# Weights, gathers and head-pair products in the expert loop of an attention and mixture-of-experts kernel: another order, and two PSUM banks at a time

## The chip, the cores and the metric

The kernel runs on one core of a Trainium2 chip. The metric is the device time of one execution in microseconds (us). A core has five engines that run at the same time and wait for each other by semaphores: PE multiplies matrices, DVE and ACT do elementwise work, POOL (GpSimd) issues most of the transfers here, and SP issues the rest. Sixteen DMA engines move the data. Each engine works through its own instructions in the order in which they are written.

## What is computed

```python
# q, k, v: 8 batches x 8 heads x 576 positions x 64; N = 4608 tokens, D = 512, E = 8 experts, F = 1024
q_s = exp(q - max_d) / sum_d                     # softmax over the 64 features
k_s = exp(k - max_s) / sum_s                     # softmax over the 576 positions
kv  = einsum('bhsd,bhse->bhde', k_s, v)          # 64 x 64 for each batch and head
x   = einsum('bhsd,bhde->bhse', q_s, kv)         # then laid out as x[N, 512]
for e in range(8):                               # the expert of a token is hash(token_ids) % 8
    out[mask_e] = relu(x[mask_e] @ w1[e]) @ w2[e]
```

## The kernel before

The kernel sorts the tokens by expert before it makes x. Each expert has 640 slots in five blocks: eight cells of 72 slots, one for each batch (576 slots, the last block holds 64 of them), and 64 overflow slots. POOL fetches the q rows of an expert by an indirect transfer for each block (`gather`, five tiles `raw`). ACT takes their exponential into `qs` (`expq`), DVE sums and scales them in two parts, blocks 0 to 2 and 3 to 4 (`sums`), PE transposes them (`turn`, into PSUM tile `pq`) and DVE copies them to `qT`. The products of `qT` with the batches' matrices `kvr` (`product`, into PSUM tile `px`) give the transposed x, and ACT and DVE, by turns, cast them to the tile `XT`. A product covers two heads (a head pair, four of them) and, in the loop, two experts at a time.

An expert is then computed in eight pieces of its first layer (`first`: 8 matmuls on `w1r` into the PSUM tile `ph`, two pieces for each of four pairs of feature rows, columns 0 to 319 and then 320 to 639), each followed by ACT's `relu` into `hT`, and five output blocks (`second`: 8 matmuls on `w2r` into `po`), each followed by DVE's `result` into one of four buffers `ob` and by POOL's indirect `scatter` of that block to the output.

Up to and with experts 0 and 1 all of this stands in one list (`ORDER`), by short names: W21 is the fetch of w1 of expert 2, S1_0 the scatter of block 0 of expert 1, A and R a piece of a first layer and its relu. Experts 2 to 7 are computed by a loop. A pass of the loop has thirteen slots, one after each of the eight pieces and the five blocks, and hangs the work for later experts into them (`sl.at(slot, ...)`, slots 0 to 7 after pieces, 8 to 12 after blocks):

- ahead of everything else in the pass: the weights of the next expert, w1 in two halves and w2 in two halves, and then the five gathers of expert e + 3;
- slots 0 to 9: sums, scaling and transposes of expert e + 2;
- in odd passes (3 and 5) slots 8 to 12: products and casts of experts e + 1 and e + 2, in three groups of cells (0 to 2, 3 to 5, 6 to 7) with four head pairs each;
- slots 8 to 12: one exponential of expert e + 3 on ACT in each.

PSUM has eight banks: `ph` takes two pairs of banks (tag S, two banks a tile), `pq` and `px` share two single banks (tag Q), and `po` has two single banks (tag T). Weights are in two sets of buffers, for even and odd experts, so that w1 of expert e + 2 can only be fetched when the first layer of expert e is through.

Of the kernel before, what the change touches and what calls it, by code (L numbers as in the profile page):

```python
# [13 lines left out]
F32 = mybir.dt.float32  # L14
F16 = mybir.dt.float16
# [275 lines left out]
class _Attention:  # L291
# [61 lines left out]

    def gather(self, idx, widths, i):
        nc = self.nc
        q16 = self.q16s[i]
        raws = []
        for i, w in enumerate(widths):
            raw = self.qpool.tile([128, D_MOE], F32, tag="qraw", bufs=10)
            nc.gpsimd.indirect_dma_start(  # L360
                out=raw[0:w, :], out_offset=None, in_=self.q[:, :],
                in_offset=bass.IndirectOffsetOnAxis(ap=idx[0:w, i:i + 1], axis=0),
                bounds_check=N_TOK - 1, oob_is_err=False)
            raws.append(raw)
        return raws, q16, widths
# [26 lines left out]

    def turn(self, rq16, i):
        nc = self.nc
        q16, w = rq16[1], rq16[2][i]
        pq = self.ps.tile([128, 512], F32, tag="Q")
        pv = pq[:].bitcast(F16).rearrange("p (r t) -> p r t", r=8)[:, 0:NPAIR, 0:w]
        for r in range(NPAIR):
            nc.tensor.transpose(pv[:, r, :], q16[0:w, i, 2 * r:2 * r + 2, :].rearrange("p h d -> p (h d)"),  # L399
                                self.ident[0:w, 0:w])  # L400
        return pv
# [37 lines left out]
class _Moe:  # L439
# [4 lines left out]

    def fetch(self, w, e, what):
        src = self.w1 if what == 1 else self.w2
        for i in range(2):
            self.nc.gpsimd.dma_start(w[what - 1][:, 2048 * i:2048 * i + 2048], src[e, :, 2048 * i:2048 * i + 2048])  # L448
# [182 lines left out]
class _Steps:  # L631
# [35 lines left out]
def kernel(  # L667
# [13 lines left out]
    with ExitStack() as fctx:  # L681
# [17 lines left out]
        with tc.manual_schedule(engines={eng.Pool, eng.PE, eng.DVE, eng.Activation}):  # L699
# [20 lines left out]

            def gather(e):
                return at.gather(ix.gidx[:, e, :], QW, e if e < 2 else 1 - e % 2)

# [32 lines left out]

            def fetch(e, what):
                if what == 1:
                    wts[e] = moe.new_weights(wb if e % 2 else wa)
                moe.fetch(wts[e], e, what)  # L760

            for e in (0, 1, 2):
                for what in (1, 2):
                    add(f"W{e}{what}", fetch, e, what)
            for e in (0, "O", 1, 2, 3, 4):
# [76 lines left out]

            def turned(rq, e, i):
                V(qT[:, :, e % 4, 128 * i:128 * i + QW[i]], at.turn(rq, i))

            for e in range(2, E_MOE):
                h, w = hs[e % 2], wts[e]
                if e + 1 < E_MOE:
                    fetch(e + 1, 1)
                    fetch(e + 1, 2)  # L850
                sl.clear()
                X = None

                def softened(ee):
                    rq = qs[ee]
                    sl.at(0, lambda: sl.at(2, at.sums(rq, 0, 3)))
                    sl.at(3, lambda: sl.at(5, at.sums(rq, 3, 5)))
                    for i, t in enumerate((5, 6, 7, 9, 9)):
                        sl.at(t, lambda i=i: turned(rq, ee, i))

                def products(ee, es, t):
                    for (lo, hi), s in zip(((0, 3), (3, 6), (6, 8)), t):
                        for r in range(NPAIR):
# [71 lines left out]
```

## Time and profile before

| | |
|---|---|
| median of 3 runs | 246.99 us (246.44 to 248.87) |
| the profiled execution | 246.38 us |
| span of its trace, first to last instruction | 244.5 us |
| PE busy | 195.6 us, 80% of the span |
| DVE, ACT, POOL busy | 139.2, 114.4 and 113.8 us |
| mean granted TensorE clock | 0.983 of 2.4 GHz |
| chain that ended last | PE 49%, DMA 33% of the span |

The profiled execution spends 1.88 us outside its span. Until about 87 us the chain runs through transfers; from there to 237.7 us it runs on PE, with a few pieces of other engines and of transfers between. The loop over experts 2 to 7 begins at 116.5 us.

### The profile page before, as it was taken

Reading aid. Unit: us, or ns where it says so; the run is one execution under the profiler, and the core shown is the slowest. Engines: PE = TensorE matmul, PEld = TensorE weight load, DVE = VectorE, ACT = ScalarE, POOL = GpSimd, SP = SyncE. Lnnn points to the kernel's source line nnn. Section 1 sums busy time; section 2 is a strip of 40 time slices with the busy share of each in tenths; the row PEclk is TensorE's granted clock in tenths of the full one; section 3 lists DMA queues with packets and bytes.
Section 4 is the critical chain, followed back from the end, with each engine's and each line's share of the span. In section 5 each row is a group of like instructions: output and inputs, shape, how many; then the busy total and the mean of one; then the engine's idle time right before and its main releaser. Section 6 shows DMA issues by size and latency. Waiting matters only on the chain.

```text
span 244.5 us, 4885 instructions
## 1 busy us (share of the span) xinstructions
PE 195.6 (80%) x1955; PEld 128.0 (52%) x1955; DVE 139.2 (57%) x274; ACT 114.4 (47%) x181; POOL 113.8 (47%) x140
## 2 busy tenths in 40 slices
PE   2536605729659989999999895799999899999980
PEld 2436605617534565665764563367557556647530
DVE  7895438291883799835854584279359552031140
ACT  8533337856951892480441650456166234505400
POOL 6170341635434628834884585068753226043051
PEclk9999999999998999999999999799999999999998
DMA  6999999999999728795599499529988924982032
GB/s 220 323 328 314 415 327 286 323 260 251 214 212 279 247 87 157 246 188 178 117 213 300 164 182 247 188 95 181 237 305 165 218 101 106 212 226 88 1 129 79
DMA packets 13548, 51.42 MB, mean 210 GB/s; under 512 B 2504, under 2 KB 2504, under 8 KB 12496
## 3 DMA queue, kind: packets, MB, share of 16 engines
q0 software_dynamic: 12224, 41.58, 68.3%
q1 hardware_dynamic: 1296, 9.47, 9.8%
q8 instruction: 17, 0.28, 0.5%
q14 instruction: 11, 0.09, 0.1%
HBM read 63.25 MB, written 10.49 MB: 302 GB/s over the span
## 4 chain that ended last, share of the span: by engine, by line
PE 49%; DMA 33%; issue 5%; DVE 5%; POOL 3%; ACT 2%; POOLq 0%; ACTq 0%; DVEq 0%
PE ph L462 22%; PE po L474 22%; DMA raw<-in_q_dram,gidx 17%; DMA v<-in_v_dram 9%; DMA w2r<-in_moe_w_dram 7%; PE px L410 3%; PE pq L399 2%; POOL raw L360 2%; DVE A L127 1%; ACT qs L371 1%; ACT hT L467 1%; DVE ob L480 1%; ACT XT L810 1%; DVE EV L107 0%; POOL w1r L448 0%
## 5 line engine op out<-in xcount | busy, mean ns | idle before, releaser
L462 PE MATMUL ph<-XT,w1r 128*128 128x320 f16 (+2 forms) x512 | 75.6, 303 | 1.1 <-ACT hT L467 1.1
L474 PE MATMUL po<-w2r,hT 128*128 128x512 f16 x320 | 75.3, 387 | 0.0
L484 POOL DMA_INDIRECT out_dram<-ob,sidx x40 | 40.5, 1013 | 66.8 <-DVE ob L480 61.1
L467 ACT ACTIVATE hT<-ph 128x640 f16<-128x640 f32 (+2 forms) x64 | 44.8, 703 | 43.4 <-PE ph L462 43.2
L480 DVE TENSOR_SCALAR ob<-po 128x512 f32<-128x512 f32 x40 | 27.6, 690 | 61.0 <-PE po L474 56.6
L462 PEld LDWEIGHTS <-w1r 128*128 128x128 f16 x512 | 49.8, 99 | 21.3 <-issue 1.6
L360 POOL DMA_INDIRECT raw<-in_q_dram,gidx x40 | 44.6, 1114 | 30.9 <-issue 6.6
L474 PEld LDWEIGHTS <-hT 128*128 128x128 f16 x320 | 30.8, 100 | 34.0 <-issue 3.1
L371 ACT ACTIVATE qs<-raw 128x512 f16<-128x512 f32 (+1 forms) x44 | 26.3, 626 | 26.5 <-DMA raw<-in_q_dram,gidx 26.3
L383 DVE TENSOR_REDUCE rq<-qs 128x16 f32<-128x1024 f16 (+1 forms) x18 | 26.1, 1450 | 5.2 <-ACT qs L371 5.1
L399 PE MATMUL pq<-ident,qs 128*128 128x128 f16 (+1 forms) x176 | 16.4, 228 | 12.8 <-DVE qs L389 11.9
L389 DVE TENSOR_TENSOR qs<-qs,rq 128x1024 f16<-128x1024 f16 (+1 forms) x18 | 26.2, 1455 | 0.3
L338 PE MATMUL pt<-v,k 64*64 64x65 f16 x576 | 15.0, 222 | 10.6 <-ACT v L328 10.6
L410 PE MATMUL px<-qT,kvr 128*128 128x144 f16 (+1 forms) x160 | 14.6, 224 | 10.8 <-ACT XT L810 4.6
L399 PEld LDWEIGHTS <-qs 128*128 128x128 f16 (+1 forms) x176 | 12.3, 103 | 17.0 <-issue 10.3
L810 ACT CAST XT<-px 128x288 f16<-128x288 f32 (+1 forms) x26 | 11.6, 453 | 20.5 <-PE px L410 20.4
L338 PEld LDWEIGHTS <-k 64*64 64x64 f16 x576 | 14.5, 136 | 11.2 <-issue 10.7
L410 PEld LDWEIGHTS <-kvr 128*128 128x128 f16 x160 | 11.5, 103 | 16.2 <-issue 11.2
L324 ACT ACTIVATE k<-kraw 128x2304 f16<-128x2304 f32 x8 | 16.9, 2118 | 2.4 <-PE pt L338 1.7
L810 DVE CAST XT<-px 128x288 f16<-128x288 f32 (+1 forms) x26 | 13.2, 518 | 6.8 <-PE px L410 6.8
L448 POOL DMA_DIRECT2D w1r<-in_moe_w_dram x16 | 9.3, 596 | 7.2 <-PE px L410 4.7
L448 POOL DMA_DIRECT2D w2r<-in_moe_w_dram x16 | 8.9, 576 | 2.3 <-DMA v<-in_v_dram 1.6
(102 smaller groups left out, 110.4 us busy)
## 6 DMA issues: line engine op xcount, KB each, us to landing
kraw<-in_k_dram SPq DMA_DIRECT2D x8, 1152.0 KB, 10.2
w1r<-in_moe_w_dram POOLq DMA_DIRECT2D x16, 512.0 KB, 7.7
w2r<-in_moe_w_dram POOLq DMA_DIRECT2D x16, 512.0 KB, 11.3
v<-in_v_dram POOLq DMA_DIRECT2D x8, 594.0 KB, 17.1
raw<-in_q_dram,gidx POOLq DMA_INDIRECT x40, 10.5
out_dram<-ob,sidx POOLq DMA_INDIRECT x40, 3.2
raw<-in_q_dram,oidx POOLq DMA_INDIRECT x4, 15.5
ids<-in_moe_token_ids_dram SPq DMA_DIRECT2D x1, 36.0 KB, 1.7
```

Source lines behind the costliest of these rows:

```text
L338: nc.tensor.matmul(pkv[s, r, 0:DH_ + 1], lhsT=k16[s, r * C9 + c, :], rhs=v16[s, r * C9 + c, 0:DH_ + 1], start=(c == 0), stop=(c == C9 - 1))
L360: nc.gpsimd.indirect_dma_start(out=raw[0:w, :], out_offset=None, in_=self.q[:, :], in_offset=bass.IndirectOffsetOnAxis(ap=idx[0:w, i:i + 1 ...
L371: self.nc.scalar.activation(q16[0:w, i].rearrange("p h d -> p (h d)"), raws[i][0:w, :], ACT.Exp)
L389: nc.vector.tensor_tensor(out=qf, in0=qf, in1=rv.rearrange("p i h -> p (i h)").unsqueeze(2) .to_broadcast([w, (hi - lo) * H_, DH_]), op=AL ...
L399: nc.tensor.transpose(pv[:, r, :], q16[0:w, i, 2 * r:2 * r + 2, :].rearrange("p h d -> p (h d)"), self.ident[0:w, 0:w])
L410: nc.tensor.matmul(pv[:, :, i * CELL:(i + 1) * CELL], lhsT=self.kvrs[b][:, r, :], rhs=qT[:, r, q0 + es.start:q0 + es.stop, b * CELL:(b + 1 ...
L462: nc.tensor.matmul(ph[:, i, :hi - lo], lhsT=w1r[:, dc, fc * 128:(fc + 1) * 128], rhs=XTp[:, e % 2, dc, lo:hi], start=(dc == 0), stop=(dc = ...
L467: self.nc.scalar.activation(hT[:, 2 * f2:2 * f2 + 2, lo:hi], ph[:, :, :hi - lo], ACT.Relu)
L474: nc.tensor.matmul(po[:], lhsT=hT[:, fc, blk * 128:(blk + 1) * 128], rhs=w2r[:, fc, :], start=(fc == 0), stop=(fc == FC - 1))
L480: self.nc.vector.tensor_scalar(out=ob[:], in0=po[:], scalar1=1.0 / SX, scalar2=None, op0=ALU.mult)
L484: sc = self.nc.gpsimd.indirect_dma_start(out=self.out[:, :], out_offset=bass.IndirectOffsetOnAxis(ap=self.ix.sidx[:, e, blk:blk + 1], axis=0),
L810: (V if r % 2 else A)(X[:, es, r, lo * CELL:hi * CELL], px[e, r, lo])
```

## The change

Five things change, all but one of them in the loop:

1. The gathers of expert e + 3 stand first in a pass, and the two halves of w2 of expert e + 1 are put between them, after the second and after the fourth gather.
2. The two halves of w1 are fetched two experts ahead (w1 of e + 2 in pass e) in slots 8 and 10, behind the scatters of blocks 0 and 2. For this, w1 of expert 3 (W31) is fetched in the list ahead of the loop, behind the last piece of expert 1's first layer and ahead of expert 1's scatters.
3. The products of the loop write two head pairs into one tile of two banks (`products`, tag S, shared with `ph`), and one cast takes both: pairs 0 and 1 by ACT, pairs 2 and 3 by DVE.
4. The groups of products stand in slots 8, 10 and 11, whole, instead of being spread over 8 to 12.
5. `turn` transposes up to two blocks into one bank, followed by one copy: blocks 0 and 1 in slot 5, block 2 in slot 6, blocks 3 and 4 in slot 8 (before: slots 5, 6, 7, 9 and 9).

The matmuls are the same in number and shape (PE has 5012 rows in both orders).

```diff
-    def gather(self, idx, widths, i):
+    def gather(self, idx, widths, i, between={}):
...
         for i, w in enumerate(widths):
+            if i in between:
+                between[i]()
...
+    def products(self, qT, h, lo, hi, es, q0):
+        nc = self.nc
+        px = self.ps.tile([128, 2, 512], F32, tag="S")
+        n, ne = hi - lo, es.stop - es.start
+        pv = px[:, :, 0:ne * n * CELL].rearrange("p r (e i) -> p e r i", e=ne)
+        for r in range(2):
+            for i in range(n):
+                b = lo + i
+                nc.tensor.matmul(pv[:, :, r, i * CELL:(i + 1) * CELL], lhsT=self.kvrs[b][:, 2 * h + r, :],
+                                 rhs=qT[:, 2 * h + r, q0 + es.start:q0 + es.stop, b * CELL:(b + 1) * CELL],
+                                 start=True, stop=True)
+        return pv
...
-PP2_01 TP3_3 EQ4_2 PC2_01 A1_0_3 TC3_3 R1_0_1 PP2_00 TP3_4 R1_0_3 A1_288_2 TC3_4 PC2_00 EQ4_0 PP2_61 PP2_60
+PP2_01 TP3_3 EQ4_2 PC2_01 A1_0_3 TC3_3 R1_0_1 PP2_00 TP3_4 R1_0_3 A1_288_2 TC3_4 W31 PC2_00 EQ4_0 PP2_61 PP2_60
...
             for e in range(2, E_MOE):
                 h, w = hs[e % 2], wts[e]
-                if e + 1 < E_MOE:
-                    fetch(e + 1, 1)
-                    fetch(e + 1, 2)
...
-                    for i, t in enumerate((5, 6, 7, 9, 9)):
-                        sl.at(t, lambda i=i: turned(rq, ee, i))
+                    for i, n, t in ((0, 2, 5), (2, 1, 6), (3, 2, 8)):
+                        sl.at(t, lambda i=i, n=n: turned(rq, ee, i, n))
...
-                        for r in range(NPAIR):
-                            sl.at(s + r // 2, lambda r=r, lo=lo, hi=hi: (
-                                prod(ee, es, r, lo, hi), prodc(ee, es, r, lo, hi)))
+                        for h in range(2):
+                            sl.at(s, lambda h=h, lo=lo, hi=hi: (A, V)[h](
+                                X[:, es, 2 * h:2 * h + 2, lo * CELL:hi * CELL],
+                                at.products(qT, h, lo, hi, es, ee % 4 - es.start)))
...
-                        products(e + 1, slice(0, 2), (8, 9, 11))
+                        products(e + 1, slice(0, 2), (8, 10, 11))
+                w2 = {2 * i + 2: lambda i=i: fetch(e + 1, 2, (i,)) for i in range(2)}
                 if e + 3 < E_MOE:
-                    qs[e + 3] = gather(e + 3)
+                    qs[e + 3] = gather(e + 3, between=w2)
+                elif e + 1 < E_MOE:
+                    for f in w2.values():
+                        f()
+                if e + 2 < E_MOE:
+                    for i in range(2):
+                        sl.at(8 + 2 * i, lambda i=i: fetch(e + 2, 1, (i,)))
```

Line numbers move: 360 becomes 362, 448 becomes 465, 484 becomes 501, 480 becomes 497, 371 becomes 373, 844 becomes 860, and the casts of the loop go from line 810 to line 877. On POOL, the queue of pass 3 in the loop, from its first instruction to its last scatter, before (`w1r` and `w2r` are weights, `raw` gathered q rows, `out_dram` the output):

```order
L448 DMA w1r<-in_moe_w_dram 128x2048 x2
L448 DMA w2r<-in_moe_w_dram 128x2048 x2
L360 DMA raw<-in_q_dram,gidx 128x512 x4
L360 DMA raw<-in_q_dram,gidx 64x512
L484 DMA out_dram<-ob,sidx 4608x512 x5
```

and the same pass on POOL now:

```order
L362 DMA raw<-in_q_dram,gidx 128x512 x2
L465 DMA w2r<-in_moe_w_dram 128x2048
L362 DMA raw<-in_q_dram,gidx 128x512 x2
L465 DMA w2r<-in_moe_w_dram 128x2048
L362 DMA raw<-in_q_dram,gidx 64x512
L501 DMA out_dram<-ob,sidx 4608x512
L465 DMA w1r<-in_moe_w_dram 128x2048
L501 DMA out_dram<-ob,sidx 4608x512 x2
L465 DMA w1r<-in_moe_w_dram 128x2048
L501 DMA out_dram<-ob,sidx 4608x512 x2
```

The first gather stood behind four halves of weights and now stands behind none of its own pass; the halves of w1 moved to stand among the scatters.

On ACT, behind the relus of pass 3, before (`qs` from `raw` is an exponential, `XT` from `px` a cast of products):

```order
L810 CAST XT0_265<-px_2352 128x2x216
L371 ACTIVATE qs1_106<-raw_2210 128x512
L810 CAST XT0_265<-px_2389 128x2x216
L810 CAST XT0_265<-px_2399 128x2x216
L371 ACTIVATE qs1_106<-raw_2214 128x512
L810 CAST XT0_265<-px_2424 128x2x216
L371 ACTIVATE qs1_106<-raw_2218 128x512
L810 CAST XT0_265<-px_2449 128x2x144
L371 ACTIVATE qs1_106<-raw_2222 128x512
L810 CAST XT0_265<-px_2472 128x2x144
L371 ACTIVATE qs1_106<-raw_2226 64x512
```

and now:

```order
L877 CAST XT0_265<-px_2356 128x2x2x216
L373 ACTIVATE qs1_106<-raw_2204 128x512
L373 ACTIVATE qs1_106<-raw_2208 128x512
L877 CAST XT0_265<-px_2405 128x2x2x216
L373 ACTIVATE qs1_106<-raw_2213 128x512
L877 CAST XT0_265<-px_2437 128x2x2x144
L373 ACTIVATE qs1_106<-raw_2217 128x512
L373 ACTIVATE qs1_106<-raw_2222 64x512
```

Six casts became three of twice the width; the second one has two exponentials ahead of it, where it had one.

On DVE, from the second output block of pass 3 on, before (`ob` from `po` is the result of a block, `qT` from `pq` a copy of transposes):

```order
L480 TENSOR_SCALAR ob_2372<-po_2363 128x512
L844 COPY qT_263<-pq_2377 128x4x128
L844 COPY qT_263<-pq_2383 128x4x64
L810 CAST XT0_265<-px_2394 128x2x216
L810 CAST XT0_265<-px_2404 128x2x216
L480 TENSOR_SCALAR ob_2419<-po_2410 128x512
```

and now, from the first output block of that pass on:

```order
L497 TENSOR_SCALAR ob_2341<-po_2332 128x512
L860 COPY qT_263<-pq_2346 128x4x192
L877 CAST XT0_265<-px_2364 128x2x2x216
L497 TENSOR_SCALAR ob_2385<-po_2376 128x512
L497 TENSOR_SCALAR ob_2400<-po_2391 128x512
L877 CAST XT0_265<-px_2413 128x2x2x216
```

The copy of blocks 3 and 4 moved from behind the second result to behind the first one, and two more results now stand between it and the cast of the second group of products.

## Rows read from the trace of the kernel before

**Rows 1.** Busy time of each engine, granted clock, DMA share: before the loop; passes 3, 4, 5.

```profile
86.90:116.46 29.56, 29.55 (x220) 18.27 (x220) 21.75 (x40) 14.97 (x27) 15.93 (x16) 1.00 0.67 169
...
135.01:162.39 27.38, 22.48 (x157) 13.94 (x156) 14.27 (x24) 11.76 (x20) 13.28 (x15) 0.94 0.69 177
162.39:180.94 18.55, 18.55 (x128) 11.24 (x125) 12.38 (x21) 9.04 (x15) 13.05 (x14) 1.00 0.91 228
180.94:202.89 21.95, 20.87 (x157) 13.39 (x156) 14.41 (x24) 8.67 (x15) 7.67 (x10) 1.00 0.68 161
```

**Rows 2.** The chain in pass 3: start, us, what.

```profile
141.87 11.37 DMA raw<-in_q_dram,gidx
...
153.32 0.63 ACT qs L371
...
154.41 0.88 PE px L410 x6
155.29 2.94 PE po L474 x8
158.23 0.38 PE px L410 x6
```

**Rows 3.** What PE waited for, 100 to 245 us: total us, times, longest.

```profile
PE px L410 <- ACT XT L810: 3.9, 2, 3.5
PE px L410 <- DVE qT L844: 1.3, 2, 0.7
PE ph L462 <- ACT hT L467: 0.8, 1, 0.8
```

**Rows 4.** Busy time, granted clock, DMA share in pass 3, right behind the long wait.

```profile
154.40:158.05 3.65, 3.64 (x14) 1.75 (x14) 0.61 (x1) 1.05 (x2) 0.00 (x0) 0.56 0.52 178
```

**Rows 5.** The chain in pass 5, columns as above.

```profile
196.36 0.64 PE px L410 x6
197.00 1.73 PE po L474 x8
```

**Rows 6.** Landing of the five gathers of pass 3, issued from 141.9 us on.

```profile
DMA to landing us min/median/max: 9.0/10.3/11.4
```

**Rows 7.** Pass 6 while weights alone are moved: DMA share, GB/s in the last columns.

```profile
210.00:212.00 2.00, 2.00 (x15) 1.32 (x14) 0.00 (x0) 1.24 (x3) 0.00 (x0) 1.00 1.06 215
```

**Rows 8.** Landing of the last of five gathers issued at 99.4 us.

```profile
DMA to landing us min/median/max: 3.5/3.5/3.5
```

**Rows 9.** Casts and exponentials by form, 116 to 205 us.

```profile
L371 ACT ACTIVATE qs<-raw 128x512 f16<-128x512 f32 x12 | 7.6, 631 | 19.3 <-DMA raw<-in_q_dram,gidx 19.1
...
L810 DVE CAST XT<-px 128x432 f16<-128x432 f32 x8 | 4.8, 603 | 5.0 <-PE px L410 5.0
...
L810 ACT CAST XT<-px 128x432 f16<-128x432 f32 x8 | 4.1, 517 | 10.8 <-PE px L410 10.8
```

**Rows 10.** Cost on POOL of issuing half of w1: busy us and mean ns of one, all 16.

```profile
L448 POOL DMA_DIRECT2D w1r<-in_moe_w_dram x16 | 9.3, 596 | 7.2 <-PE px L410 4.7
```

**Rows 11.** Landing of the scatter of block 0 of expert 2, issued at 128.7 us.

```profile
DMA to landing us min/median/max: 8.5/8.5/8.5
```

**Rows 12.** DVE in order of time: last result of expert 1, scaling and last result of pass 2.

```profile
116.66 0.69 DVE L480 TENSOR_SCALAR ob<-po 128x512 f32<-128x512 f32 x1 [1.03 <-PE po L474]
...
119.59 1.76 DVE L389 TENSOR_TENSOR qs<-qs,rq 128x1536 f16<-128x1536 f16 x1
...
123.75 1.21 DVE L389 TENSOR_TENSOR qs<-qs,rq 128x1024 f16<-128x1024 f16 x1
...
137.37 0.69 DVE L480 TENSOR_SCALAR ob<-po 128x512 f32<-128x512 f32 x1 [3.20 <-PE ph L462]
```

**Rows 13.** Scatter of block 0 of expert 1: issue and landing.

```profile
L484 POOL DMA_INDIRECT out_dram<-ob,sidx x1: 1028/1028/1028, 109.7 to 109.7; - x1
...
DMA to landing us min/median/max: 3.7/3.7/3.7
```

**Rows 14.** PE in order of time, pass 2: its first transposes.

```profile
122.98 0.39 PE L399 MATMUL pq<-ident,qs 128*128 128x128 f16 x4
```

More of the change, by code (lines that the diff above doesn't have):

```diff
@@ L391, in sums, with turn @@
         return scale
-    def turn(self, rq16, i):
+    def turn(self, rq16, i, n=1):
         nc = self.nc
-        q16, w = rq16[1], rq16[2][i]
+        q16, w = rq16[1], rq16[2]
         pq = self.ps.tile([128, 512], F32, tag="Q")
-        pv = pq[:].bitcast(F16).rearrange("p (r t) -> p r t", r=8)[:, 0:NPAIR, 0:w]
-        for r in range(NPAIR):
-            nc.tensor.transpose(pv[:, r, :], q16[0:w, i, 2 * r:2 * r + 2, :].rearrange("p h d -> p (h d)"),
-                                self.ident[0:w, 0:w])
-        return pv
+        pv = pq[:].bitcast(F16).rearrange("p (r t) -> p r t", r=NPAIR)
+        for j in range(i, i + n):
+            o = 128 * (j - i)
+            for r in range(NPAIR):
+                nc.tensor.transpose(pv[:, r, o:o + w[j]], q16[0:w[j], j, 2 * r:2 * r + 2, :]
+                                    .rearrange("p h d -> p (h d)"), self.ident[0:w[j], 0:w[j]])
+        return pv[:, :, 0:sum(w[i:i + n])]
     def product(self, qT, r, lo, hi, es, q0=0):
@@ L443, in __init__, with fetch @@
         self.out, self.ix, self.ps = out, ix, ps
-    def fetch(self, w, e, what):
+    def fetch(self, w, e, what, halves=(0, 1)):
         src = self.w1 if what == 1 else self.w2
-        for i in range(2):
+        for i in halves:
             self.nc.gpsimd.dma_start(w[what - 1][:, 2048 * i:2048 * i + 2048], src[e, :, 2048 * i:2048 * i + 2048])
@@ L719, with gather @@
             ix.core(cpool, lambda: at.fill(ix))
-            def gather(e):
-                return at.gather(ix.gidx[:, e, :], QW, e if e < 2 else 1 - e % 2)
+            def gather(e, **kw):
+                return at.gather(ix.gidx[:, e, :], QW, e if e < 2 else 1 - e % 2, **kw)
             st = _Steps()
@@ L755, with fetch @@
             add("GO", lambda: qs.update(O=at.gather(oidx, [128] * NBP, 0)))
-            def fetch(e, what):
-                if what == 1:
+            def fetch(e, what, halves=(0, 1)):
+                if e not in wts:
                     wts[e] = moe.new_weights(wb if e % 2 else wa)
[L760 to L764, printed above, removed]
+                moe.fetch(wts[e], e, what, halves)
+            for e, what in ((0, 1), (0, 2), (1, 1), (1, 2), (2, 1), (2, 2), (3, 1)):
+                add(f"W{e}{what}", fetch, e, what)
             for e in (0, "O", 1, 2, 3, 4):
@@ L841, with turned @@
             sl = _Slots()
-            def turned(rq, e, i):
-                V(qT[:, :, e % 4, 128 * i:128 * i + QW[i]], at.turn(rq, i))
+            def turned(rq, e, i, n):
+                V(qT[:, :, e % 4, 128 * i:128 * i + sum(QW[i:i + n])], at.turn(rq, i, n))
             for e in range(2, E_MOE):
                 h, w = hs[e % 2], wts[e]
-                if e + 1 < E_MOE:
-                    fetch(e + 1, 1)
-                    fetch(e + 1, 2)
                 sl.clear()
@@ L857, in softened @@
                     sl.at(3, lambda: sl.at(5, at.sums(rq, 3, 5)))
-                    for i, t in enumerate((5, 6, 7, 9, 9)):
-                        sl.at(t, lambda i=i: turned(rq, ee, i))
+                    for i, n, t in ((0, 2, 5), (2, 1, 6), (3, 2, 8)):
+                        sl.at(t, lambda i=i, n=n: turned(rq, ee, i, n))
                 def products(ee, es, t):
                     for (lo, hi), s in zip(((0, 3), (3, 6), (6, 8)), t):
-                        for r in range(NPAIR):
-                            sl.at(s + r // 2, lambda r=r, lo=lo, hi=hi: (
-                                prod(ee, es, r, lo, hi), prodc(ee, es, r, lo, hi)))
+                        for h in range(2):
+                            sl.at(s, lambda h=h, lo=lo, hi=hi: (A, V)[h](
+                                X[:, es, 2 * h:2 * h + 2, lo * CELL:hi * CELL],
+                                at.products(qT, h, lo, hi, es, ee % 4 - es.start)))
                 if e + 2 < E_MOE:
@@ L869 @@
                         X = XTs[(e + 1) // 2 % 2]
-                        products(e + 1, slice(0, 2), (8, 9, 11))
+                        products(e + 1, slice(0, 2), (8, 10, 11))
+                w2 = {2 * i + 2: lambda i=i: fetch(e + 1, 2, (i,)) for i in range(2)}
                 if e + 3 < E_MOE:
-                    qs[e + 3] = gather(e + 3)
+                    qs[e + 3] = gather(e + 3, between=w2)
[5 more added lines that the diff above has]
+                        sl.at(8 + 2 * i, lambda i=i: fetch(e + 2, 1, (i,)))
+                if e + 3 < E_MOE:
                     for i in range(5):
```

## The prediction

> **What bounds the kernel now.** I read the busy time by stretch first. In the 29.56 us ahead of the loop PE is busy for 29.55 [rows 1], so nothing is to be had there but by less work on PE. In the loop, pass 4 keeps PE busy for all of its 18.55 us; passes 3 and 5 take 27.38 and 21.95 us [rows 1]. They hold the same pieces and blocks and, on top, the products: 32 matmuls. Six of those take 0.38 us [rows 2], so 32 take 2.0 us, and an odd pass without a wait would take 18.55 + 2.0 = 20.55 us. Pass 3 is 6.83 us above that and pass 5 is 1.40 us: 8.2 us in which PE stands or crawls. All else in the loop is PE at work.
>
> The list of PE's waits says for what: casts of products by ACT (3.9 us, one of 3.5), copies of transposes by DVE (1.3 us, two waits) and a relu (0.8) [rows 3]. The chain names the cause of the largest. The first gather of pass 3 is under way for 11.37 us, the exponential that waits for it starts at 153.32, and only behind it can ACT cast the products whose bank PE needs for the next ones, at 154.41 [rows 2]. The wait has a tail: right behind it the granted clock is 0.56 of full speed, a mix of the 1.2 and 2.4 GHz levels [rows 4]; the next block takes 2.94 us where one takes 1.73 [rows 2, 5], and six products 0.88 instead of 0.38 [rows 2]: 1.7 us. Adding up pass 3: 0.8 + 0.7 + 3.5 + 1.7 = 6.7, the 6.83 to within the small gaps. The relu that PE waits for early in this pass stands on ACT behind late exponentials too, those of pass 2's gathers.
>
> **The change part by part.**
>
> *Gathers first.* In pass 3 the five gathers land 9.0 to 11.4 us after issue [rows 6]: they are issued behind four halves of weights, which are moved first. A half is 512 KB; where weights alone are moved they go at 215 GB/s [rows 7], 2.44 us a half, 9.8 us for four. The last gather of an earlier group, issued when the weights ahead of it were through, landed in 3.5 us [rows 8]. Now the first two gathers have no weights of their own pass ahead of them, the last has two halves: between 3.5 and 3.5 + 2 x 2.44 = 8.4 us. They are also issued sooner, since four issues of weights at 0.6 us [rows 10] no longer stand ahead. POOL is through with the last scatter of expert 2 some 2 us after PE begins pass 3 at 135.0, so the first two go out by 138.5 and the last, with three gathers and two halves between, at about 143.5; they land by about 144 (3.5 us and one half left over) and 152. ACT needs the first two when PE comes to the third group of products, which reuses the banks of the second: 9.9 us of pieces and transposes (18.55 less five blocks of 1.73), four blocks and two groups, so from 135.0 + 9.9 + 6.9 + 1.5 = 153.3, and less a cast, 152. It needs the last at the end of the pass, 135.0 + 20.55 = 155.6. That leaves 8 and 3.6 us. So the 3.5 us, the 1.7 us of low clock behind it and the 0.8 go. Nothing on ACT is late in their place: it is busy for 11.76 us of this pass [rows 1].
>
> *Transposes in slots 5, 6, 8.* The two waits for DVE were for the copy of blocks 3 and 4, made in slot 9 directly ahead of the products that read it. The copy now comes in slot 8, two blocks or 3.5 us ahead. Slot 8 needs the scaling of blocks 3 and 4, over at 123.75 + 1.21 = 124.96 in pass 2 [rows 12], and comes after the pieces and one block, at about 127.7. One of these waits is in pass 3, the other in pass 5; there 3.9 - 3.5 = 0.4 us for ACT's cast between groups [rows 3] goes with it, as the groups no longer stand directly behind one another in two banks. Worth the 1.4 us of pass 5 and the 0.7 already counted in pass 3.
>
> *Two head pairs a cast.* ACT takes 0.517 and DVE 0.603 us for 432 columns [rows 9]. A cast of 864 is at most two of these, 1.03 and 1.21, and not less than one. I take the upper end, which costs nothing: between the groups in slots 10 and 11 lies a block of 1.73 us, in which ACT has one exponential (0.63 [rows 9]) and a cast (1.03). DVE has a result (0.69 [rows 12]) and a cast (1.21) in 1.73 + 0.75. The two-bank tiles are shared with the first layer: the products of slot 8 wait for the last relus, and the next pass's first pieces for the casts of slot 11, each with a block between. The matmuls are the same. Value 0, between 0 and +1.2 (four handovers at 0.3, if that cover fails).
>
> *w1 among the scatters.* Two halves, 1.2 us of POOL's time [rows 10], now stand between five scatters of 1.03 us [rows 13]: 6.4 us in the 8.65 of five blocks. Their own wait is for a first layer that is over. Each scatter behind a half lands up to 2.44 us later. A buffer `ob` is used again after four blocks, so block 4 waits for the scatter of block 0. That happened before: the scatter of expert 2's block 0 took 8.5 us [rows 11], and DVE began block 4's result only at 137.37 [rows 12], without a wait of PE for it. Now it has two halves ahead, not four, issued sooner. Value 0.
>
> *W31 ahead of the loop.* Here something gets worse. On POOL W31 waits for expert 1's last piece, with expert 1's scatters behind it; that piece is over well before their first result. But w1 of expert 3 is now moved ahead of those scatters. The one of block 0 landed at 109.7 + 3.7 = 113.4 [rows 13]; two more halves make that 118.3. The last result of expert 1 needs its buffer and began at 116.66 [rows 12], so DVE starts pass 2's sums 1.6 us late. The scaling that ended at 119.59 + 1.76 = 121.35 [rows 12] then ends at 123.0; PE transposes at 122.98 [rows 14]. The slack just covers it: +0.1, between 0 and +1.2 (if a half takes 3 us).
>
> Sum: -6.8 - 1.4 + 0.1 = -8.1 us against the profiled execution of 246.38: **238.3 us**. That execution is 0.6 us below the median; the forecast stays with it, and the difference goes into the range. The end of the program (the last scatter) is not touched.
>
> **The rivals.**
>
> *DMA becomes the bound.* Pass 4 has a DMA share of 0.91 over 18.55 us [rows 1]: 16.9 us of work, and passes 2 to 4 now follow at 18.55, 20.55 and 18.55. For it: only 1.7 us are to spare in an even pass. Against it: the work per pass stays the same and is spread more evenly. If the mix runs 20% slower, a pass needs 20.3 us, and passes 2 and 4 lose 1.7 each: 241.7. The Trainium skill (DMA: Bandwidth & Descriptors, Specifications) gives a limit of about 358 GB/s of HBM traffic for a core; by it a half, read as 1 MB of fp32, would take an estimated 2.9 us, an even pass's transfers some 18.3 us, the queue would hardly ever run empty, and this rival would have 0.3. The trace does not bear it out: 215 GB/s written in 16 bit [rows 7] is 430 GB/s read.
>
> *The change does not do what it says: the gathers stay late.* If they take 11.4 us [rows 6] still, the second lands at 150 and the last at 155, and each of three passes loses up to 1 us: 239.5 to 241. Against it: the 3.5 us [rows 8].
>
> *The shared banks bind.* If exponentials come in a burst, ACT has two (1.26) and a cast (1.03) ahead of the products of slot 11, 2.3 us in 1.73: 0.6 at each handover, 239.3 to 240.7.
>
> *Slower than before: scatters.* If the scatters of block 0 are held up among the weights, DVE, which works in order, waits for a buffer, and the sums for the next transposes are late. It decides from about 8.5 us of landing: 6.9 us (four blocks) until the buffer is needed and 1.6 us of slack. At 13 us, half as much again as the worst seen [rows 11], each of passes 2 to 4 would lose 4.5 us and 1.7 of low clock behind it, as in pass 3: 238.3 + 3 x 6.2 = 256.9. Against it: with all four halves ahead it was 8.5.
>
> **How the numbers follow.** The forecast, all waits gone but for tenths, has 0.76 (237.4 to 239.2); late gathers 0.08; shared banks 0.06; DMA 0.06; scatters 0.02; anything else 0.02. The runs before reach 2.4 us above their lowest. The range, with these cases and the ends of the unknown costs, is 237.2 to 241.4. One per cent, 2.5 us, is about what a measurement of this kernel can tell from no change. All but the last two cases gain more than that: faster 0.95, same 0.03, slower 0.02.
>
> **What would show it.** In the profile after: passes 3 and 5 at about 20.5 us each with PE busy throughout; no wait of PE for casts or copies of over 0.3 us; gathers landing in 3 to 8 us; no granted clock below 1.00 in the loop; pass 2 at 18.5 to 19.7; casts of 864 columns at 1.0 to 1.2 us. The prediction is wrong if pass 2 or 4 grows by over a microsecond (DMA or W31), or if ACT still waits for gathers between its casts.

## Result and profile after

The changed kernel takes 240.32 us in the median of 4 runs (239.44 to 242.1), the kernel before 247.93 (246.44 to 249.55, 4 runs). The ratio is 0.970, with an interval from 0.961 to 0.979. The profiled execution took 239.44 us with a span of 237.7, against 246.38 and 244.5 before. Here and below a ratio leaves out the executions that ran in a slower state of the chip (over 1.5% above the fastest of the same kernel).

The first view to read is the busy time by stretch, for passes 2 to 5 and for what follows the last matmul. The columns are busy us of PE, PE's weight loads, DVE, ACT and POOL, then granted clock, DMA share and GB/s.

```profile
116.66:136.70 20.04, 18.71 (x125) 11.16 (x124) 11.38 (x16) 8.56 (x13) 13.27 (x15) 1.00 0.76 199
136.70:157.25 20.55, 20.55 (x158) 13.24 (x156) 14.48 (x19) 10.65 (x16) 14.91 (x15) 1.00 1.02 244
157.25:175.79 18.54, 18.54 (x125) 11.25 (x124) 11.98 (x18) 7.93 (x12) 13.67 (x14) 1.00 0.91 206
175.79:196.55 20.76, 20.71 (x158) 13.24 (x156) 14.32 (x19) 8.66 (x12) 8.04 (x10) 1.00 0.88 202
...
231.30:237.70 6.40, 0.07 (x1) 0.00 (x0) 0.69 (x1) 0.00 (x0) 1.30 (x2) 0.67 0.22 78
```

Against [rows 1], pass 3 went from 27.38 to 20.55 us and pass 5 from 21.95 to 20.76, with PE busy throughout; pass 4 stayed; the granted clock is 1.00 in all four. Pass 2, which runs from 116.46 to 135.01 before, 18.55 us, grew to 20.04, and there PE is idle for 1.33 us. From the start of the loop to the end of the span it is 121.04 us, 128.04 before. The sum: -6.83 (pass 3), -1.19 (pass 5), +1.49 (pass 2), -0.5 (the end, 6.90 us before), and the loop begins 0.2 us later: -6.8, which is 237.7 - 244.5.

What PE waited for from 100 us on, the view that answers to [rows 3], has one row left:

```profile
PE pq L403 <- DVE qs L391: 1.3, 1, 1.3
```

The four casts and copies of [rows 3] and the relu are gone from it. The one new wait is for DVE's scaling. Its cause is in the chain of waits in pass 2 (start, us, what):

```profile
109.92 9.87 DMA out_dram<-ob,sidx
...
119.92 0.69 DVE ob L497
120.61 1.67 DVE rq L385
...
122.85 1.77 DVE qs L391
...
124.67 0.62 PE pq L403 x8
```

The scatter of block 0 of expert 1 (S1_0) is under way for 9.9 us, where it took 3.7 before [rows 13]; DVE's last result of expert 1 needs its buffer `ob` and begins at 119.92 instead of 116.66 [rows 12]; sums and scaling follow, and then the transposes, late.

The gathers of pass 3, which landed 9.0 to 11.4 us after issue [rows 6], now do so in

```profile
DMA to landing us min/median/max: 5.7/6.4/7.8
```

and the casts by form, from 116 to 200 us, answer to [rows 9] (busy us and mean ns of one, then idle time before and what ended it):

```profile
L877 DVE CAST XT<-px 128x864 f16<-128x864 f32 x4 | 4.2, 1058 | 0.4
L877 ACT CAST XT<-px 128x864 f16<-128x864 f32 x4 | 3.5, 879 | 9.4 <-PE px L426 9.4
```

### The profile page after: what moved, and what is told of

Read it like the earlier page. It is cut to its first block, busy times and chain, and to the rows that moved or that the text cites. A ratio compares the mean times of both kernels' runs of the same rounds, so it can differ in the third digit from the quotient of the medians.

```text
span 237.7 us, 4865 instructions
## 1 busy us (share of the span) xinstructions
PE 196.2 (83%) x1955; PEld 128.7 (54%) x1955; DVE 138.2 (58%) x260; ACT 113.3 (48%) x175; POOL 116.9 (49%) x140
## 4 chain that ended last, share of the span: by engine, by line
PE 55%; DMA 24%; DVE 9%; issue 4%; ACT 4%; POOL 2%; POOLq 0%; DVEq 0%; ACTq 0%
PE po L491 24%; PE ph L479 23%; DMA raw<-in_q_dram,gidx 14%; DMA v<-in_v_dram 5%; DMA out_dram<-ob,sidx 4%; PE pq L403 3%; DVE rq L385 2%; ACT k L324 2%; PE px L426 2%; POOL raw L362 2%; PE pt L338 2%; DVE qs L391 1%; DVE A L127 1%; DMA ids<-in_moe_token_ids_dram 1%; ACT qs L373 1%
## 5 line engine op out<-in xcount | busy, mean ns | idle before, releaser
L491 PE MATMUL po<-w2r,hT 128*128 128x512 f16 x320 | 74.3, 384 | 0.0
L362 POOL DMA_INDIRECT raw<-in_q_dram,gidx x40 | 46.7, 1169 | 30.6 <-DVE row L162 6.6
L338 PEld LDWEIGHTS <-k 64*64 64x64 f16 x576 | 15.0, 139 | 10.9 <-issue 10.4
L414 PE MATMUL px<-qT,kvr 128*128 128x72 f16 (+1 forms) x96 | 8.0, 215 | 5.4 <-DVE XT L826 3.0
L414 PEld LDWEIGHTS <-kvr 128*128 128x128 f16 x96 | 6.3, 103 | 8.5 <-issue 6.0
L877 ACT CAST XT<-px 128x864 f16<-128x864 f32 (+1 forms) x6 | 4.8, 799 | 11.9 <-PE px L426 11.9
L465 POOL DMA_DIRECT2D w2r<-in_moe_w_dram x16 | 9.4, 594 | 2.1 <-DMA v<-in_v_dram 1.6
L345 DVE TENSOR_SCALAR rec<-pt 128x4 f32<-128x4 f32 x8 | 1.3, 162 | 15.2 <-PE pt L338 15.1
```

The lines of the kernel that those rows point to most:

```text
L338: nc.tensor.matmul(pkv[s, r, 0:DH_ + 1], lhsT=k16[s, r * C9 + c, :], rhs=v16[s, r * C9 + c, 0:DH_ + 1], start=(c == 0), stop=(c == C9 - 1))
L362: nc.gpsimd.indirect_dma_start(out=raw[0:w, :], out_offset=None, in_=self.q[:, :], in_offset=bass.IndirectOffsetOnAxis(ap=idx[0:w, i:i + 1 ...
L491: nc.tensor.matmul(po[:], lhsT=hT[:, fc, blk * 128:(blk + 1) * 128], rhs=w2r[:, fc, :], start=(fc == 0), stop=(fc == FC - 1))
```

## The experiments

The stretch ahead of the loop is not a fit measure for effects of one or two microseconds: with the same instructions up to W31 it took between 116.4 and 120.5 us in the profiled executions of these kernels. So they are compared by the lengths of passes in the trace (PE's time from one first piece to the next) and by the time from the start of the loop to the end of the span. That last column holds the end of the program too, behind the last matmul, which took 6.0 to 7.4 us in these traces, and 6.0 and 6.7 in the two of one and the same kernel (W31 behind the scatters). Expectations below that name a span or a time to the end are missed by these two stretches even where the passes are as expected. In passes 2 to 5 the granted clock is 1.00 in every kernel but the one before and the one with three buffers. All in us:

| kernel | pass 2 | pass 3 | pass 4 | pass 5 | loop to end |
|---|---|---|---|---|---|
| before | 18.55 | 27.38 | 18.55 | 21.95 | 128.04 |
| after | 20.04 | 20.55 | 18.54 | 20.76 | 121.04 |
| after, again | 20.00 | 20.55 | 18.54 | 20.76 | 121.04 |
| W31 behind the scatters | 18.54 | 20.55 | 18.55 | 20.75 | 119.16 |
| the same, again | 18.55 | 20.54 | 18.70 | 20.76 | 119.97 |
| six buffers `ob` | 18.68 | 20.55 | 18.55 | 20.75 | 119.41 |
| old queue | 18.55 | 24.20 | 18.55 | 22.85 | 125.55 |
| old products and slots | 18.55 | 21.95 | 18.55 | 21.95 | 122.07 |
| new slots, old products | 18.55 | 22.26 | 18.55 | 22.20 | 123.35 |
| old slots, new products | 20.08 | 20.54 | 18.55 | 20.75 | 120.64 |
| w1 one expert ahead | 18.54 | 20.55 | 18.68 | 20.75 | 119.89 |
| three buffers `ob` | 20.75 | 26.53 | 19.36 | 27.45 | 136.22 |

All start from the changed kernel. Ratios are to the kernel before on the same chip.

### W31 behind the scatters

```diff
-... TP3_4 R1_0_3 A1_288_2 TC3_4 W31 PC2_00 ... S1_0 ... S1_4
+... TP3_4 R1_0_3 A1_288_2 TC3_4 PC2_00 ... S1_0 ... S1_4 W31
```

> W31 goes behind the last scatter of expert 1, so that w1 of expert 3 no longer stands ahead of those scatters. Theory (the scatter of block 0 lands late behind w1, the last result of expert 1 waits for its buffer, DVE starts pass 2 late and PE waits 1.3 us for the scaling): the last result begins at about 116.7 instead of 119.9, pass 2 falls from 20.04 to 18.55 us and the span from 237.7 to 236.2; the gathers of pass 2 land up to 4.9 us later, which nothing waits for. Rival (pass 2 is longer because paired transposes in slot 5 need the scaling earlier, or because the transfers are crowded as such): pass 2 stays at 19.5 to 20 us, span 237.5 or more.

Measured: 240.61 us (240.21 to 241.22, 4 runs), ratio 0.966 (0.957 to 0.975). Pass 2 is back at 18.54 us and the list of PE's waits in the loop is empty. The span is 238.4 us and not the 236.2 expected, above all since the loop began at 119.2 us and not at 116.7. DVE in order of time, the last result of expert 1 (in brackets its idle time before and what ended it), in this kernel:

```profile
119.44 0.69 DVE L497 TENSOR_SCALAR ob<-po 128x512 f32<-128x512 f32 x1 [1.03 <-PE po L491]
```

and in the changed kernel:

```profile
119.92 0.69 DVE L497 TENSOR_SCALAR ob<-po 128x512 f32<-128x512 f32 x1 [4.09 <-DMA out_dram<-ob,sidx]
```

With W31 ahead, the result waits for the scatter's transfer; with it behind, for PE's block alone, as before [rows 12]. That w1 of expert 3 is fetched later cost pass 3 nothing.

### Six buffers for results

```diff
-        opool = P("o", 4)
+        opool = P("o", 6)
```

> Six result buffers instead of four, all else as in the changed kernel. Theory (it is the buffer that is waited for): the scatter of expert 1's block 0 still lands some 10 us after issue, but the last result no longer waits for it; pass 2 is 18.55 us and the span 236.2. Rival (crowded transfers or late scaling as such): pass 2 stays at 20 us.

Measured: 240.8 us (240.32 to 241.12, 4 runs), ratio 0.965 (0.957 to 0.974); pass 2 at 18.68 us, no wait of PE in the loop. Here W31 stands where the change put it, and the same result does not wait:

```profile
120.00 0.69 DVE L497 TENSOR_SCALAR ob<-po 128x512 f32<-128x512 f32 x1 [1.03 <-PE po L491]
```

So W31 does its harm through the buffer that S1_0 keeps, and hardly by holding up anything else (0.13 us of pass 2 are left).

### The old queue with the new products

```diff
+                if e + 1 < E_MOE:
+                    fetch(e + 1, 1)
+                    fetch(e + 1, 2)
...
-                    qs[e + 3] = gather(e + 3, between=w2)
+                    qs[e + 3] = gather(e + 3)
...
-                if e + 2 < E_MOE:
-                    for i in range(2):
-                        sl.at(8 + 2 * i, lambda i=i: fetch(e + 2, 1, (i,)))
```

W31 is out as well.

> The order of the POOL queue of the kernel before (w1 and w2 of the next expert, then the gathers; no W31), with the paired products and the new transposes. Theory (the queue order is worth the 6 us in which ACT waits for gathers and PE for ACT): gathers land 8 to 12 us after issue again, pass 3 is 25 to 27 us with a granted clock below 1.00 behind a wait of over 3 us, pass 5, which has no gathers, stays at 20.6 and pass 2 goes to 18.55; span 241.5 to 243. Rival (the paired products alone take the waits away, since a cast no longer stands between each two groups): pass 3 is under 22 us and the span under 238.

Measured: 244.47 us (243.51 to 247.1, 5 runs), ratio 0.979 (0.970 to 0.988). What PE waited for in the loop:

```profile
PE px L426 <- ACT XT L880: 2.8, 1, 2.8
PE ph L479 <- ACT hT L484: 2.5, 2, 1.9
```

and the chain in pass 3:

```profile
146.31 12.34 DMA raw<-in_q_dram,gidx
...
158.73 0.63 ACT qs L373
159.36 0.78 ACT XT L880
...
160.18 0.66 PE px L426 x8
160.84 1.73 PE po L491 x8
```

This is [rows 2] over again: a gather under way for more than 11 us, an exponential, a cast, and PE waits for the cast's banks. The new products make the wait shorter, 2.8 instead of 3.5 us, and do not remove it. The relus add 0.6 us in pass 3 and 1.9 in pass 5: on ACT they stand behind exponentials of late gathers. One thing is missing against before: the clock behind the wait stays at 1.00 (more on this below), so the 1.7 us of low clock is not paid. The expectation missed both odd passes: 24.20 us for pass 3 where it had 25 to 27, and 22.85 for pass 5 where it had 20.6, since it left out the relus.

### Old products and old slots with the new queue

```diff
-                    for i, n, t in ((0, 2, 5), (2, 1, 6), (3, 2, 8)):
-                        sl.at(t, lambda i=i, n=n: turned(rq, ee, i, n))
+                    for i, t in enumerate((5, 6, 7, 9, 9)):
+                        sl.at(t, lambda i=i: turned(rq, ee, i, 1))
...
-                        for h in range(2):
-                            sl.at(s, lambda h=h, lo=lo, hi=hi: (A, V)[h](
-                                X[:, es, 2 * h:2 * h + 2, lo * CELL:hi * CELL],
-                                at.products(qT, h, lo, hi, es, ee % 4 - es.start)))
+                        for r in range(NPAIR):
+                            sl.at(s + r // 2, lambda r=r, lo=lo, hi=hi: (
+                                prod(ee, es, r, lo, hi), prodc(ee, es, r, lo, hi)))
...
-                        products(e + 1, slice(0, 2), (8, 10, 11))
+                        products(e + 1, slice(0, 2), (8, 9, 11))
```

> The new POOL queue with the transposes in slots 5, 6, 7, 9, 9 and the products by single head pairs in single banks, as before. Theory (the copy of blocks 3 and 4 and the two single banks cost PE 1.4 us in each odd pass, whatever the gathers do): passes 3 and 5 are both 21.9 to 22.2 us, with PE waiting 0.7 for the copy and 0.4 for a cast in each; span 240.3 to 240.8. Rival (these waits came from late gathers as well): passes 3 and 5 at 20.5 to 21, span 238.

Measured: 244.95 us (242.5 to 247.12, 4 runs), ratio 0.979 (0.963 to 0.994). Passes 3 and 5 both take 21.95 us, as pass 5 did before; this is the changed queue by itself. PE's waits in the loop:

```profile
PE px L414 <- DVE qT L860: 1.3, 2, 0.7
PE px L414 <- issue: 0.8, 2, 0.4
```

The 1.3 us for copies is the second row of [rows 3], unchanged. The other row is 0.4 us in each odd pass, where PE waited for ACT's cast in pass 5 before ([rows 3], 3.9 less 3.5); here the profile shows nothing that it waits for. A second reading comes for nothing: pass 2 takes 18.55 us here although W31 stands ahead of the scatters, and DVE shows why:

```profile
122.29 0.69 DVE L497 TENSOR_SCALAR ob<-po 128x512 f32<-128x512 f32 x1 [2.60 <-DMA out_dram<-ob,sidx]
```

The result waited 2.60 us, 1.6 more than the 1.03 of [rows 12], and PE did not wait. In the changed kernel it waited 4.09, 3.1 more, and PE lost 1.33. So the slack is at least the 1.6 us that the prediction had; what came out otherwise is the scatter. Here S1_0 was issued at 113.8 and the result that waits for it began 8.5 us later; in the changed kernel it took 9.9 us to land, with the same instructions ahead of it on POOL. In both kernels two more scatters stand right behind it. In the changed one the DMA engines move 195 GB/s from 112 to 117 us and 385 GB/s from 117 to 119, and then the first three scatters land within 1.3 us, at 119.8, 120.4 and 121.1: S1_0 was not moved alone. Why it came through earlier here, no run tells.

### New slots for the transposes, old products

```diff
-                        for h in range(2):
-                            sl.at(s, lambda h=h, lo=lo, hi=hi: (A, V)[h](
...
+                        for r in range(NPAIR):
+                            sl.at(s + r // 2, lambda r=r, lo=lo, hi=hi: (
+                                prod(ee, es, r, lo, hi), prodc(ee, es, r, lo, hi)))
...
-                        products(e + 1, slice(0, 2), (8, 10, 11))
+                        products(e + 1, slice(0, 2), (8, 9, 11))
```

> The new queue and the new transposes (slots 5, 6, 8), with products by single pairs in single banks, in slots 8, 9 to 12. Theory (of the 1.4 us that an odd pass lost, the waits for the copy of blocks 3 and 4 and for the cast have separate causes: the copy's place and the two single banks): no wait for a copy, but 0.4 us and hand-over for a cast between the batches remains, so passes 3 and 5 are 20.9 to 21.3 us. Rival (the paired products alone take both away): passes 3 and 5 stay at 21.9 as with the old transposes.

Measured: one run, 244.61 us. Passes 3 and 5 take 22.26 and 22.20 us: not the 20.9 to 21.3 of my theory, but no gain at all on 21.95. PE's waits in the loop:

```profile
PE px L414 <- ACT XT L826: 2.1, 4, 0.6
PE px L414 <- DVE XT L826: 0.3, 2, 0.2
```

and PE in order of time in pass 3 (in brackets the idle time before, and what ended it):

```profile
150.65 0.35 PE L414 MATMUL px<-qT,kvr 128*128 128x144 f16 x3 [0.61 <-ACT XT L826]
...
153.52 0.35 PE L414 MATMUL px<-qT,kvr 128*128 128x144 f16 x3 [0.42 <-ACT XT L826]
...
154.02 0.35 PE L414 MATMUL px<-qT,kvr 128*128 128x144 f16 x3 [0.16 <-DVE XT L826]
```

The wait for the copies is gone, as it should be, and PE waits for casts instead: four head pairs pass through two single banks, and a product waits until a bank has been cast. The first of these waits, 0.61 us, is new: it comes in slot 8, where the transposes of blocks 3 and 4 now stand directly ahead of the products and share their two banks.

### Old slots for the transposes, new products

The other half, with the two-bank products left in slots 8, 10 and 11:

```diff
-                    for i, n, t in ((0, 2, 5), (2, 1, 6), (3, 2, 8)):
-                        sl.at(t, lambda i=i, n=n: turned(rq, ee, i, n))
+                    for i, t in enumerate((5, 6, 7, 9, 9)):
+                        sl.at(t, lambda i=i: turned(rq, ee, i, 1))
```

> The changed kernel with the transposes block by block in slots 5, 6, 7, 9, 9 as before; queue and paired products as changed. The experiment with new transposes and single banks lost 1.7 us a pass, so the earlier theory (the copy's place is a cause of its own) fell; the new one is that two-bank tiles, with the second group a block later, are what removes both waits. Then passes 3 and 5 are 20.5 to 20.8 us here and no wait for a copy is left, since the copy of slot 9 has a block of 1.73 us before the products of slot 10. If the copy's place matters as well, passes 3 and 5 are 21.2 us or more.

Measured: one run, 238.82 us. PE's waits in the loop:

```profile
PE pq L403 <- DVE qs L391: 1.4, 1, 1.4
```

That is W31's wait in pass 2 alone. Passes 3 and 5 take 20.54 and 20.75 us, as with the new slots. The transposes' slots are worth nothing here; the products make the gain.

### w1 one expert ahead

```diff
-                w2 = {2 * i + 2: lambda i=i: fetch(e + 1, 2, (i,)) for i in range(2)}
+                w1 = {2 * i + 2: lambda i=i: fetch(e + 1, 1, (i,)) for i in range(2)}
...
-                if e + 2 < E_MOE:
+                if e + 1 < E_MOE:
                     for i in range(2):
-                        sl.at(8 + 2 * i, lambda i=i: fetch(e + 2, 1, (i,)))
+                        sl.at(8 + 2 * i, lambda i=i: fetch(e + 1, 2, (i,)))
```

W31 is out: pass 2 fetches w1 of expert 3 itself.

> The gathers stand first, but the halves between them are of w1 of the next expert, and the halves among the scatters are of w2 of the next expert; nothing is fetched two experts ahead and there is no W31. Theory (what matters is that the gathers are ahead of the weights and that the weights are spread; two experts ahead is only one way to have room): w1 lands some 13 us into a pass, w2 some 3 us into the next, both before they are needed, so all passes are as in the version with W31 behind the scatters, 119.0 us from the start of the loop to the end. Rival (w1 must come two experts ahead): PE waits for w1 at the start of passes 3 to 7 or for w2 at their first blocks, over 1 us each, 123 us or more.

Measured: 241.87 us (240.39 to 242.35, 7 runs), ratio 0.965 (0.960 to 0.970). Busy time in passes 2 and 3:

```profile
118.71:137.25 18.54, 18.54 (x125) 11.24 (x124) 11.54 (x16) 8.16 (x13) 14.11 (x15) 1.00 0.74 173
137.25:157.80 20.55, 20.55 (x158) 13.24 (x156) 14.49 (x19) 11.04 (x17) 14.77 (x15) 1.00 0.99 242
```

PE stands in neither. Two experts ahead are not needed. What this kernel has in common with the changed one is that the gathers stand ahead of most of the weights and that the weights are spread over the pass; no run has one of the two without the other, so which of them counts is not shown. The loop to the end takes 119.89 us where 119.0 was expected; of the 0.7 us more than with W31 behind the scatters 0.6 are the end of the program.

### The changed kernel and W31 behind the scatters, again

Both once more, on another chip, without an edit.

> The changed kernel once more, beside the next three on one chip. By the theory its pass 2 is 18.55 us plus what the last result of expert 1 is late beyond 1.6 us of slack; it was 3.1 us late in the first trace (1.5 us lost) and 1.6 us late in the experiment with the old products (nothing lost), so pass 2 is 18.5 to 20.1 us and the time 0 to 1.5 us above the version with W31 behind the scatters. A rival that puts pass 2's length down to anything else would have it at 20.0 again with the result less than 1.6 us late.

> W31 behind expert 1's scatters, once more, beside the changed kernel: all passes without a wait of PE but for some 0.3 us in pass 5; from the start of the loop to the end of the span 119.0 us, against 119 to 121 of the changed kernel; the median 0 to 1.5 us below that of the changed kernel.

Measured: 241.99 us (240.78 to 244.22, 6 runs), ratio 0.966 (0.960 to 0.972), and 241.15 (240.32 to 242.12, 6 runs), ratio 0.962 (0.957 to 0.967). The medians differ by 0.84 us in the expected direction, but the intervals overlap: by time alone it isn't settled. From the start of the loop to the end the second kernel takes 119.97 us and not the 119.0 expected; pass 4 and the end of the program are 0.15 and 0.65 us longer than in its first trace. Pass 2 repeats itself: it takes 20.00 us with W31 ahead,

```profile
119.16:139.16 20.00, 18.72 (x125) 11.17 (x124) 11.38 (x16) 8.56 (x13) 13.30 (x15) 1.00 0.76 200
```

and 18.55 with it behind:

```profile
120.23:138.78 18.55, 18.55 (x126) 11.25 (x125) 11.53 (x16) 8.14 (x12) 15.07 (x17) 1.00 0.91 213
```

### Three buffers for results

```diff
-        opool = P("o", 4)
+        opool = P("o", 3)
```

> Three result buffers instead of four, all else as in the changed kernel: how far the scatters, which now stand behind halves of w1 and land some 7 us after issue, are from holding up PE. With three buffers a result waits for the scatter three blocks back, so DVE is some 3 us late at the end of each pass with weights and gathers; of that 1.6 us are covered. Theory of the slower rival (a late scatter delays DVE, DVE the scaling, the scaling PE's transposes): passes 2 to 5 grow by 1 to 3 us each over the changed kernel, PE waiting for the scaling in slot 5. If the scatters have room to spare, the passes are as in the changed kernel, but for pass 2.

Measured: one run, 254.8 us, span 253.0. PE's and then DVE's waits in the loop:

```profile
PE pq L403 <- DVE qs L391: 11.2, 4, 4.4
```

```profile
DVE ob L497 <- DMA out_dram<-ob,sidx: 24.3, 6, 6.5
```

The mechanism of the prediction's slower rival is a real one: with a buffer fewer, DVE stands for 24.3 us at results whose buffer a scatter still holds, the sums behind it are late, and PE waits 11.2 us for the scaling. With four buffers the changed kernel has none of that from pass 3 on. The expectation of 1 to 3 us a pass fits neither kind of pass: against the changed kernel passes 2 and 4 grow by 0.7 and 0.8 us, passes 3 and 5 by 6.0 and 6.7, of which a part is low clock (see the last section).

## Why the prediction was right, point by point

The forecast was 238.3 us; the profiled execution, against which the sum was made, took 239.44, and the median of 240.32 lies in the range. The sum was -8.1 us, measured was -6.9. The sign and the main cause held; one term was mis-sized beyond its bound, one gain was put down to the wrong edit, and 0.5 us came unforeseen. That the total is only 1.1 us off is in part luck: W31 cost 1.4 us more than forecast, and the shorter end gave 0.5 back.

*Gathers first: the right mechanism, somewhat overvalued.* Pass 3 was to lose 6.8 us and lost 6.83. Of the 6.8 the prediction gave 6.0 to the gathers (3.5, 1.7 and 0.8) and 0.7 to the transposes. The new queue alone, with old products and slots, takes 5.43 us off pass 3 (27.38 to 21.95); the other 1.40 comes with the new products. The gathers landed in 5.7 to 7.8 us, within the 3.5 to 8.4 worked out, and no low clock is left in the loop. Putting back the old queue brings the chain of [rows 2] back, with pass 3 at 24.20. Over passes 2 to 5, the queue alone makes 5.4 us (86.43 to 81.00), the products and slots alone 2.3 (to 84.15, old queue). Together they would make 7.7; less the 1.49 that W31 costs in pass 2 that is 6.2, near the 6.5 measured (to 79.89).

*Transposes in slots 5, 6, 8: the step that failed.* The prediction gave them the 1.4 us of pass 5. Alone they gain nothing (22.26 and 22.20 us), and without them nothing is lost (20.54 and 20.75). The wait for the copy was read correctly from [rows 3], but I asked too little what comes next: single banks stand behind it, and PE then waits for casts. The prediction did name the 0.4 us of ACT's cast there and let it go with the rest, "as the groups no longer stand directly behind one another"; that parting is the products' doing, not the transposes'. No wait of PE for casts or copies of over 0.3 us is left, as the prediction had it, but by another edit than the one it named.

*Two head pairs a cast: undervalued.* They were set at 0 and make the odd passes' gain: with the new queue, passes 3 and 5 go from 21.95 to 20.54 and 20.75 by the products alone. The two-bank tiles and the slots of their groups (8, 10, 11 for 8, 9, 11) were changed together, and no run parts them. Since the sum counted the 1.4 us once, it stayed right in size for a wrong reason. The costs were in bounds: casts of 864 take 0.879 and 1.058 us, against at most 1.03 and 1.21 (where the prediction says what would show it, it has 1.0 to 1.2 us; ACT's are below).

*w1 among the scatters: right* at 0 from pass 3 on, with four buffers; three are too few.

*W31 ahead of the loop: the right mechanism, mis-sized.* The prediction put the landing of S1_0 at 118.3, its result 1.6 us late and the cost at +0.1, at most 1.2. Pass 2 grew by 1.49 us to 20.04, above the 18.5 to 19.7 given for it and by more than the microsecond that the prediction itself had named as a sign of being wrong. The scatter was issued at 109.9 and took

```profile
DMA to landing us min/median/max: 9.9/9.9/9.9
```

so the buffer came free at 119.8, not 118.3, and the last result waited 3.1 us longer than before, against a slack of about 1.6: +1.49. Adding two halves at 2.44 us to 3.7 gives 8.6, which is what the kernels with the old products show (8.5 at most); the other 1.3 us the sum did not have. The trace shows three scatters landing within 1.3 us of each other there, while the sum had the first one alone; that this is the cause is not tested, and with the old products the first of three took only 8.5. Moving W31 behind the scatters takes the 1.49 away, two buffers more all but 0.13 of it.

*Not forecast:* the end of the program, from the last matmul's time on, took 6.40 us instead of 6.90. Two traces of one kernel differ by more (6.0 and 6.7 us), so this is not shown to come from the change.

*Left over:* pass 5 is 0.2 us longer than pass 3. The chain of waits in pass 5 of the changed kernel shows where:

```profile
175.96 3.27 PE ph L479 x24
...
179.27 0.33 issue
179.60 0.71 ACT hT L484
...
180.35 2.33 PE ph L479 x16
```

A relu begins 0.33 us after what released it, with nothing in the profile that it waits for. The same gap stands at the same place in the kernels with two-bank products (all but the one with three buffers, whose chain runs elsewhere), and not in the two with single-bank products. Its cause stays open.

*The rivals.* Late scatters were the one that came in part: S1_0 in pass 2 is its mechanism, once and for 1.33 us. DMA did not become the bound: pass 3 has a DMA share of 1.02 and pass 4 one of 0.91, and PE stands in neither. The gathers did not stay late. The shared banks do not bind: no wait of PE for `px` or `XT` is left.

A better version is in reach: with W31 behind the scatters, with six buffers, or with w1 one expert ahead, the loop to the end takes 119.2 to 120.0 us instead of 121.04. By the medians these three lie within a microsecond of the changed kernel, so the gain is shown by the passes of the trace (pass 2 falls from 20.0 to between 18.5 and 18.7) and not by the time.

## What to carry to other kernels

A transfer that an engine waits for soon belongs ahead of bulk transfers on the same queue, with the bulk spread behind it; the two together, without any other edit to the loop, were worth 5.4 us here, and how much of that is the order and how much the spreading no run tells. A transfer moved forward has to be costed at all that stands behind it on its queue: W31 held a scatter, the scatter a buffer, the buffer a result, and the result sums that PE needed. When a wait is read from a list, ask what stands directly behind it at the same place, and give the gain to an edit only when that edit has been run alone.

## What the runs showed of the hardware

The clock did not fall behind every long wait. In the kernel with the old queue PE waited 2.76 us in pass 3, and the granted clock behind it stayed at 1.00; with three buffers it waited 4.36 us, and over the next 3.5 us it was 0.56, as behind the 3.46 us before [rows 4]. The windows of these two kernels, in that order:

```profile
160.20:162.50 2.30, 2.30 (x17) 1.35 (x17) 0.76 (x1) 2.11 (x4) 0.00 (x0) 1.00 0.22 87
```

```profile
148.50:152.00 3.50, 3.43 (x22) 2.44 (x23) 3.40 (x7) 0.23 (x1) 2.88 (x4) 0.56 0.68 156
```

PE in order of time in the second shows the price, eight matmuls of the first layer at the low and at the high level:

```profile
149.40 2.34 PE L479 MATMUL ph<-XT,w1r 128*128 128x320 f16 x8
...
151.79 1.25 PE L479 MATMUL ph<-XT,w1r 128*128 128x320 f16 x8
```

How long a transfer takes is here for the most part what stands ahead of it. In the kernel before, the scatters issued from 105.1 to 117.6 us, six of them, show the spread (five landings are on record):

```profile
DMA to landing us min/median/max: 2.6/2.7/7.8
```

The 7.8 is the last scatter of expert 0, right behind the two halves of w2 of expert 2. The 3.7 of [rows 13] is the next one, issued at 109.7 us, and it had no free queue either: the second of those halves landed at 112.4, and the scatter at 113.4. The last three, issued at 113.9, 115.9 and 117.6 with those weights through, took 2.7, 2.7 and 2.6 us. With W31's two halves ahead as well it is 9.9 us in the changed kernel, and 8.5 at most in the one with old products and slots. The Trainium skill (DMA: Bandwidth & Descriptors, Anatomy of one DMA — SWDGE (gpsimd) path) fits one transfer as about 2.0 us and its bytes over 436 GB/s; for the 256 KB of a block that is an estimated 2.6 us. The last three scatters agree with it; the 9.9 do not: as a fit for one transfer it leaves out the queue.

A cast from two banks costs little less than two from one: on ACT 879 ns against 2 x 517, on DVE 1058 against 2 x 603, so 155 and 148 ns are saved with each.
